# A new token order, a new order within the step, a new prologue, and one PSUM bank moved from one pool to another, in a fused sparse attention and MLP kernel

## The chip, the core and the metric

The kernel runs on one core of a Trainium2 chip. The metric is the time of one execution on the device, in microseconds (us), taken from repeated runs. The time before is 422.28 us (median of three runs, 421.58 to 422.75). The profiler names the engines PE (TensorE, matmuls), PEld (TensorE's weight loads, which overlap PE), DVE (VectorE), ACT (ScalarE), POOL (GpSimd, which issues the loads here) and SP (the queue that issues the stores).

## The reference, cut to what matters

```python
# q, k, v: (8 batches, 8 heads, 576 tokens, 64), float32
scores = (q @ k^T) / 8
mask_local   = 0 <= i - j < 32                       # heads 0 to 3
mask_strided = i >= j and i % 32 == j % 32           # heads 4 to 7
attn = softmax(where(mask, scores, -1e9)) @ v
x = attn as (4608 tokens, 512)
h = x @ w_in                                         # 512 -> 2048: "L1"
g = where(h > 0, h, exp(min(h, 0)) - 1)              # elu
out = g @ w_out                                      # 2048 -> 512: "L2"
```

## The kernel before

Attention is done by pairs of heads: per batch two strided pairs (`hp` 2 and 3), then two local ones (`hp` 0 and 1). A pair is three *pieces*: **T** transposes q and k on TensorE into a PSUM tile each, which VectorE copies to `qT` and `kT`; two **S** pieces compute the scores of one half each, take exp on ScalarE and multiply by the mask on VectorE. After each S comes its **PV**: TensorE computes the row sums (`s_ps`) and the unnormalized output (`o_ps`), ScalarE computes 1/s_ps as exp(-ln s_ps), and VectorE writes `xT = o_ps * rc`, bf16. `xT` holds the tokens as columns and is the moving operand of L1. For the strided heads a token number is 8 * row + slot (72 rows, 8 slots). 32 tokens are four rows, so tokens of different slots never attend to each other.

The main loop has 9 x 16 steps. Each computes one L1 block of 128 hidden units for 512 tokens (four matmuls of 512 columns) and a quarter of an L2 block of the previous 512 tokens (four more). One piece of attention is placed in each step until the pieces run out.

```python
p_s = tile_pool("ps_s", bufs=1, PSUM)    # scores, two banks
p_a = tile_pool("ps_a", bufs=2, PSUM)    # shared: transposes "tp", o_ps, s_ps
p_h = tile_pool("ps_h", bufs=2, PSUM)    # L1
p_o = tile_pool("ps_o", bufs=2, PSUM)    # L2
...
def piece_O(P, u, pm):                   # PV
    o_ps = p_a.tile([128, W], F32, tag="a")
    s_ps = p_a.tile([128, W], F32, tag="a")
    ... matmuls into s_ps, then into o_ps ...
    nc.scalar.activation(ln, s_ps, ACT.Ln)
    nc.scalar.activation(rc, ln, ACT.Exp, scale=-1.0)
    xs = xT[:, P.hp, P.b * S:(P.b + 1) * S]
    if P.str:      # columns are token numbers: rows p are 8 elements apart
        dst = xs.rearrange("c (p u sp z) -> c u z sp p", u=2, sp=2, z=2)[:, u]
        nc.vector.tensor_mul(dst, o_ps..., rc...)
    else:
        nc.vector.tensor_mul(xs[:, u * W:(u + 1) * W], o_ps, rc)
...
def run_piece(p):                        # the piece, then PV of the S before it
    old = list(pend); pend.clear()
    if u < 0: piece_T(...)
    else:     pend.append((..., piece_S(...)))
    for a in old: piece_O(*a)
...
for nb in range(NCH):                    # 9 blocks of 512 tokens
    for m in range(MC):                  # 16 steps
        run_piece(pieces[done]) ...      # if any is left
        l1(nb, m)
        if nb > 0: l2(nb - 1, m)
```

The softmax here doesn't subtract the row's maximum and nothing guards it: scores larger than these inputs give would overflow.

Of the kernel before, what the change touches and what calls it, by code (L numbers as in the profile page):

```python
# [9 lines left out]
F32 = mybir.dt.float32  # L10
BF16 = mybir.dt.bfloat16
# [17 lines left out]
def kernel(  # L29
# [22 lines left out]
    p_wk = ctx.enter_context(tc.tile_pool(name="work", bufs=3))  # L52
    p_g = ctx.enter_context(tc.tile_pool(name="g", bufs=2))
    p_s = ctx.enter_context(tc.tile_pool(name="ps_s", bufs=1, space=bass.MemoryType.PSUM))
    p_a = ctx.enter_context(tc.tile_pool(name="ps_a", bufs=2, space=bass.MemoryType.PSUM))
    p_h = ctx.enter_context(tc.tile_pool(name="ps_h", bufs=2, space=bass.MemoryType.PSUM))
    p_o = ctx.enter_context(tc.tile_pool(name="ps_o", bufs=2, space=bass.MemoryType.PSUM))

    ctx.enter_context(tc.manual_schedule())

# [7 lines left out]
            out=t, in_=src[b, HG:2 * HG].rearrange("h (p s) d -> p h (s d)", s=NS))  # L68
        return t

    def load_loc(src, b, name):

        t = p_in.tile([LQ, 2, LB, 2, D], BF16, tag=name, name=name)
        for h in range(HG):
            nc.gpsimd.dma_start(  # L75
                out=t[:, h // 2, :, h % 2, :],
                in_=src[b, h].rearrange("(t p) d -> p t d", p=LQ))
        return t
# [11 lines left out]
    def load_batch(b):  # L90
        t = {}
        t["qs"] = load_str(q, b, "qs")
        t["ks"] = load_str(k, b, "ks")
        t["vs"] = load_str(v, b, "vs")
        t["ql"] = load_loc(q, b, "ql")
        t["kl"] = load_loc(k, b, "kl")
        t["vl"] = load_vloc(b)
        return t

    batch_in = {}  # L100
    batch_in[0] = load_batch(0)

    w_in_sb = weights.tile([128, KC, d_ff], BF16, tag="w_in_sb")
    w_out_sb = weights.tile([128, MC, d_model], BF16, tag="w_out_sb")
    w_in_v = moe_w_in.rearrange("(kc p) f -> p kc f", p=128)
    w_out_v = moe_w_out.rearrange("(mc p) f -> p mc f", p=128)
    xT = weights.tile([128, KC, n_tokens], BF16, tag="xT")


    identity = consts.tile([128, 128], BF16, tag="identity")  # L110
# [4 lines left out]
    )  # L115
    ones = consts.tile([128, D], BF16, tag="ones")
    nc.vector.memset(ones, 1.0)



# [7 lines left out]
    mask_s = consts.tile([RS, RS], BF16, tag="mask_s")  # L128
    nc.vector.scalar_tensor_tensor(mask_s, dist, float(RS), eq, op0=ALU.is_ge, op1=ALU.mult)


    mask_l = consts.tile([128, LB, LQ], BF16, tag="mask_l")
    nc.vector.memset(mask_l, 1.0)
    nc.gpsimd.affine_select(
        mask_l, mask_l, compare_op=ALU.is_ge, fill=0.0,
        base=-1, pattern=[[0, LB], [-1, LQ]], channel_multiplier=1)
    nc.gpsimd.affine_select(
        mask_l, mask_l, compare_op=ALU.is_ge, fill=0.0,
        base=PRE, pattern=[[0, LB], [1, LQ]], channel_multiplier=-1)
    nc.vector.memset(mask_l[0:PRE, 0, :], 0.0)  # L140

    NT = 3
    KW = PRE + S - RS + 128
    kTs = [consts.tile([128, KW], BF16, tag=f"kT{i}", name=f"kT{i}") for i in range(NT)]
    qTs = [consts.tile([128, S], BF16, tag=f"qT{i}", name=f"qT{i}") for i in range(NT)]
    for t in kTs:
        nc.vector.memset(t[:, 0:PRE], 0.0)
        nc.vector.memset(t[:, PRE + S:], 0.0)

    for i in range(4):  # L150
        nc.gpsimd.dma_start(out=w_in_sb[:, :, i * 512:(i + 1) * 512],
# [22 lines left out]
    def piece_T(P):  # L174



        for nm, dst in (("q", P.qT[:, 0:S]), ("k", P.kT[:, PRE:PRE + S])):
            ps = p_a.tile([128, S], BF16, tag="a", name="tp")
            if P.str:  # L180
                src = batch_in[P.b][nm + "s"]
                for x in range(2):
                    for sp in range(NS // 2):
                        o = (x * (NS // 2) + sp) * RS
                        nc.tensor.transpose(  # L185
                            ps[:, o:o + RS],
                            src[:, P.g0 + x, 2 * sp * D:2 * (sp + 1) * D],
                            identity[0:RS, 0:RS])
            else:
                src = batch_in[P.b][nm + "l"]  # L190
                for t in range(LB):
                    nc.tensor.transpose(  # L192
                        ps[:, t * LQ:(t + 1) * LQ],
                        src[:, P.g0 // 2, t].rearrange("p h d -> p (h d)"),
                        identity[0:LQ, 0:LQ])
            nc.vector.tensor_copy(dst, ps)  # L196

    W = S // 2

    def piece_S(P, u):  # L200

        sc = p_s.tile([128, 2, 512], F32, tag="s", name="sc")
        pm = p_wk.tile([128, 2, W], BF16, tag="pm", name="pm")
        e = p_wk.tile([128, 2, W], BF16, tag="e", name="e")
        for i in range(4 if P.str else 3):
            for z in range(2):
                pr = slice(z * D, (z + 1) * D)
                if P.str:
                    x, sp = divmod(i, 2)
                    n = RS  # L210
                    o = (x * (NS // 2) + 2 * u + sp) * RS
                    k0 = PRE + o
                else:
                    n = LQ
                    o = (3 * u + i) * LQ
                    k0 = o
                nc.tensor.matmul(  # L217
                    sc[:, z, i * n:(i + 1) * n], lhsT=P.kT[pr, k0:k0 + 128],
                    rhs=P.qT[pr, o:o + n], start=True, stop=True)
        R = RS if P.str else 128  # L220
        nc.scalar.activation(e[0:R], sc[0:R, :, 0:W], ACT.Exp, scale=scale)  # L221
        if P.str:
            nc.vector.tensor_mul(  # L223
                pm[0:R].rearrange("p z (i n) -> p (z i) n", n=RS),
                e[0:R].rearrange("p z (i n) -> p (z i) n", n=RS),
                mask_s.unsqueeze(1).to_broadcast([RS, 8, RS]))
        else:
            mb = mask_l[:, 3 * u:3 * u + 3].rearrange("p b n -> p (b n)")
            nc.vector.tensor_mul(pm, e, mb.unsqueeze(1).to_broadcast([128, 2, W]))  # L229
        return pm  # L230

    def piece_O(P, u, pm):
# [36 lines left out]
        nc.scalar.activation(rc, ln, ACT.Exp, scale=-1.0)  # L269
        xs = xT[:, P.hp, P.b * S:(P.b + 1) * S]  # L270
        if P.str:

            dst = xs.rearrange("c (p u sp z) -> c u z sp p", u=2, sp=2, z=2)[:, u]
            pat = "c (z sp p) -> c z sp p"
            nc.vector.tensor_mul(dst, o_ps.rearrange(pat, z=2, sp=2),  # L275
                                 rc.rearrange(pat, z=2, sp=2))
        else:
            nc.vector.tensor_mul(xs[:, u * W:(u + 1) * W], o_ps, rc)  # L278


    pieces = []
    for b in range(B):
        for hp in (2, 3, 0, 1):
            pieces.append((b, hp, -1))
            for u in range(2):
                pieces.append((b, hp, u))
    pend = []
    cur = [None]

    def flush():  # L290
        while pend:
            P, u, pm = pend.pop(0)
            piece_O(P, u, pm)

    def run_piece(p):
        b, hp, u = p
        old = list(pend)
        pend.clear()
        if u < 0:
            cur[0] = make_pair(b, hp)  # L300
            piece_T(cur[0])
        else:
            pm = piece_S(cur[0], u)
            pend.append((cur[0], u, pm))
        for a in old:
            piece_O(*a)


    g_of = {}
# [1 line left out]
    def l1(nb, m):  # L311
# [14 lines left out]
                                op0=ALU.min, op1=ALU.subtract)  # L326
        nc.vector.tensor_tensor(g[:, m, :], e1, hps, op=ALU.max)  # L327

    o_cur = [None]

    def l2(nb, step):

        kk, part = divmod(step, 4)
        g = g_of[nb]
        if part == 0:
            o_cur[0] = p_o.tile([128, d_model], F32, tag="o", name="ops")
        ops = o_cur[0]
        for m in range(part * 4, part * 4 + 4):
            nc.tensor.matmul(  # L339
                ops, lhsT=g[:, m, kk * 128:(kk + 1) * 128],  # L340
                rhs=w_out_sb[:, m, :], start=(m == 0), stop=(m == MC - 1))
        if part == 3:
            o_sb = p_wk.tile([128, d_model], F32, tag="osb", name="osb")
            nc.scalar.copy(o_sb, ops)  # L344
            r0 = nb * CHUNK + kk * 128
            nc.sync.dma_start(out=out[r0:r0 + 128, :], in_=o_sb)


    n_p = len(pieces) // B
    done = 0  # L350
    while done < n_p:
        run_piece(pieces[done])
        done += 1
    AHEAD = 2
    for _ in range(AHEAD):
        run_piece(pieces[done])
        done += 1
    loaded = 2
    for nb in range(NCH):
        for m in range(MC):  # L360
            if done < len(pieces):
                run_piece(pieces[done])
                done += 1
            else:
                flush()
            l1(nb, m)
            if nb > 0:
                l2(nb - 1, m)
            if done % n_p == 6 and loaded < B and loaded <= done // n_p + 1:
                batch_in[loaded] = load_batch(loaded)  # L370
                loaded += 1
    for m in range(MC):
        l2(NCH - 1, m)


# [28 lines left out]
```

## Time and profile before

| stretch | us | what it is |
|---|---|---|
| 0 to 44.3 | 44.3 | fill: attention of batch 0 (and two pieces of batch 1) until the first L1 |
| 44.3 to 93.4 | 49.1 | first block: 16 steps with a piece and L1, no L2 |
| 93.4 to 297.6 | 204.2 | mixed: 67 steps with L1, L2 and attention |
| 297.6 to 402.9 | 105.3 | pure: 61 steps with L1 and L2 only |
| 402.9 to 421.6 | 18.7 | last L2 block, last copy and store |

The stretches are cut where the timeline shows the first L1, the first L2, the end of the last attention step, and the last L1. Here is the page of the kernel before (busy us and share of the span, and two of its rows of 40 equal slices, where a digit is tenths).

```profile
span 421.6 us, 6645 instructions
PE 345.6 (82%) x2584; PEld 171.2 (41%) x2624; DVE 271.7 (64%) x501; ACT 196.7 (47%) x373; POOL 88.9 (21%) x120
PE   0256776678888878888887888888999999999996
PEclk9999988989988998998999889899999999999999
```

The windows view of the same kernel gives the busy time of each engine in four of these stretches. The columns are the stretch, its length, PE, PEld, DVE, ACT and POOL busy, the granted TensorE clock, the DMA share, and GB/s.

```profile
0.00:44.30 44.30, 16.96 (x226) 13.08 (x228) 17.30 (x43) 14.73 (x29) 30.42 (x46) 1.00 1.33 139
44.30:93.40 49.10, 35.11 (x321) 17.88 (x326) 37.37 (x69) 24.00 (x49) 19.70 (x26) 0.89 1.39 126
93.40:297.60 204.20, 173.98 (x1494) 85.98 (x1516) 147.40 (x266) 109.24 (x214) 38.77 (x49) 0.93 0.46 55
297.60:402.90 105.30, 104.83 (x480) 47.73 (x488) 68.27 (x123) 45.19 (x76) 0.00 (x0) 1.00 0.10 38
```

Only the pure steps are bound by TensorE: it is busy 104.83 of 105.30 us, and a step takes 105.3 / 61 = 1.73 us. In the mixed steps nothing is full: TensorE idles for 30 us (about 4 of them only look idle, because 22 matmul records are missing from the trace), VectorE for 57, and the clock is 0.93. A busy average of 85% doesn't say what to do; the order of waits does. One T step on the timeline of the kernel before shows it (start, duration, engine, line, operation, output<-input; in brackets the engine's idle time just before, and what ended it).

```profile
202.68 1.45 DVE L275 TENSOR_TENSOR xT<-o_ps,rc 128x288 bf16<-128x288 f32 x1 [0.32 <-ACT rc L269]
203.23 0.42 PE L192 MATMUL tp<-identity,ql 96*128 96x96 bf16 x6
...
204.18 0.41 PE L192 MATMUL tp<-identity,kl 96*128 96x96 bf16 x6 [0.53 <-DVE xT L275]
...
205.06 0.42 DVE L196 COPY qT_130<-tp 128x576 bf16<-128x576 bf16 x1
205.39 0.45 DVE L196 COPY kT_127<-tp 128x576 bf16<-128x576 bf16 x1
205.53 0.31 PE L240 MATMUL s_ps<-pm,ones 72*64 72x288 bf16 x2 [0.94 <-DVE qT_130 L196]
...
205.89 0.32 PE L249 MATMUL o_ps<-pm,vs 72*64 72x72 bf16 x8
```

The K transposes (line 192, `kl`) wait for xT of the PV before, because that PV's `o_ps` holds one of the two shared banks. Then both shared banks hold transposes, so `s_ps` waits for the Q copy and `o_ps` for the K copy. L1, which needs neither, stands behind them in TensorE's queue and starts only at 206.37.

The groups view of the kernel before shows the two xT writes (count, busy us, mean ns, idle before). They move the same 128 x 288 elements.

```profile
L275 DVE TENSOR_TENSOR xT<-o_ps,rc 128x288 bf16<-128x288 f32 x32 | 46.0, 1437 | 20.0 <-ACT rc L269 20.0
L278 DVE TENSOR_TENSOR xT<-o_ps,rc 128x288 bf16<-128x288 f32 x32 | 14.6, 458 | 19.0 <-ACT rc L269 19.0
```

Line 275, the strided one, puts one bf16 into every 16 bytes and takes 1437 ns instead of 458.

### The profile page before, as it was taken

Reading aid. Unit: us, or ns where it says so; the run is one execution under the profiler, and the core shown is the slowest. Engines: PE = TensorE matmul, PEld = TensorE weight load, DVE = VectorE, ACT = ScalarE, POOL = GpSimd, SP = SyncE. Lnnn points to the kernel's source line nnn. Section 1 sums busy time; section 2 is a strip of 40 time slices with the busy share of each in tenths; the row PEclk is TensorE's granted clock in tenths of the full one; section 3 lists DMA queues with packets and bytes.
Section 4 is the critical chain, followed back from the end, with each engine's and each line's share of the span. In section 5 each row is a group of like instructions: output and inputs, shape, how many; then the busy total and the mean of one; then the engine's idle time right before and its main releaser. Section 6 shows DMA issues by size and latency. Waiting matters only on the chain.

```text
span 421.6 us, 6645 instructions
## 1 busy us (share of the span) xinstructions
PE 345.6 (82%) x2584; PEld 171.2 (41%) x2624; DVE 271.7 (64%) x501; ACT 196.7 (47%) x373; POOL 88.9 (21%) x120
## 2 busy tenths in 40 slices
PE   0256776678888878888887888888999999999996
PEld 0234433334433434443443344344444444444442
DVE  0265687786777777677777666776766666666620
ACT  1135454545644644564564446456543434444421
POOL 7847347404310530341051000000000000000000
PEclk9999988989988998998999889899999999999999
DMA  9999999925942964498296000000010101010111
GB/s 106 108 205 138 188 147 133 110 40 53 89 83 55 80 66 79 43 84 103 55 82 63 24 3 26 26 25 26 26 47 29 52 25 50 26 50 26 51 50 75
DMA packets 81502, 28.97 MB, mean 69 GB/s; under 512 B 65856, under 2 KB 76864, under 8 KB 81472
## 3 DMA queue, kind: packets, MB, share of 16 engines
q0 software_dynamic: 76288, 19.12, 49.7%
q1 hardware_dynamic: 5184, 9.44, 5.9%
q8 instruction: 20, 0.33, 0.3%
q14 instruction: 10, 0.08, 0.1%
HBM read 38.21 MB, written 9.44 MB: 113 GB/s over the span
## 4 chain that ended last, share of the span: by engine, by line
PE 61%; DVE 15%; DMA 9%; ACT 6%; issue 4%; POOL 4%; POOLq 0%; ACTq 0%
PE hps L318 28%; PE ops L339 27%; DVE xT L275 4%; DVE g L327 4%; DMA ks<-in_k_dram 3%; DMA qs<-in_q_dram 3%; PE sc L217 3%; ACT he L323 2%; DMA vs<-in_v_dram 2%; PE o_ps L261 1%; ACT e L221 1%; ACT rc L269 1%; PE o_ps L249 1%; PE s_ps L256 1%; ACT osb L344 1%
## 5 line engine op out<-in xcount | busy, mean ns | idle before, releaser
L318 PE MATMUL hps<-xT,w_in_sb 128*128 128x512 bf16 x542 | 152.4, 403 | 5.5 <-issue 5.2
L339 PE MATMUL ops<-w_out_sb,g 128*128 128x512 bf16 x570 | 151.0, 392 | 0.4
L323 ACT ACTIVATE he<-hps 128x512 f32<-128x512 f32 x144 | 85.8, 596 | 87.3 <-PE hps L318 84.4
L339 PEld LDWEIGHTS <-g 128*128 128x128 bf16 x576 | 58.0, 101 | 72.6 <-issue 8.2
L318 PEld LDWEIGHTS <-w_in_sb 128*128 128x128 bf16 x576 | 51.4, 101 | 58.5 <-issue 8.0
L221 ACT ACTIVATE e<-sc 72x576 bf16<-72x576 f32 (+1 forms) x64 | 41.4, 648 | 42.6 <-PE sc L217 41.3
L275 DVE TENSOR_TENSOR xT<-o_ps,rc 128x288 bf16<-128x288 f32 x32 | 46.0, 1437 | 20.0 <-ACT rc L269 20.0
L267 ACT ACTIVATE ln<-s_ps 128x288 f32<-128x288 f32 x64 | 26.1, 407 | 68.9 <-PE s_ps L240 39.1
L75 POOL DMA_DIRECT2D ql<-in_q_dram x32 | 23.6, 747 | 38.4 <-PE tp L192 27.2
L344 ACT COPY osb<-ops 128x512 f32<-128x512 f32 x36 | 21.1, 585 | 20.0 <-PE ops L339 20.0
L269 ACT ACTIVATE rc<-ln 128x288 f32<-128x288 f32 x64 | 28.3, 443 | 2.0
L75 POOL DMA_DIRECT2D kl<-in_k_dram x32 | 23.8, 755 | 16.5 <-DMA qs<-in_q_dram 6.2
L278 DVE TENSOR_TENSOR xT<-o_ps,rc 128x288 bf16<-128x288 f32 x32 | 14.6, 458 | 19.0 <-ACT rc L269 19.0
L240 PE MATMUL s_ps<-pm,ones 72*64 72x288 bf16 x64 | 11.0, 330 | 15.0 <-DVE qT_131 L196 4.9
L256 PE MATMUL s_ps<-pm,ones 128*64 128x288 bf16 x64 | 10.8, 327 | 13.2 <-DVE qT_130 L196 4.8
L223 DVE TENSOR_TENSOR pm<-e,mask_s 72x576 bf16<-72x576 bf16 x32 | 14.7, 459 | 8.2 <-ACT e L221 8.2
L185 PE MATMUL tp<-identity,qs 72*128 72x72 bf16 x128 | 7.7, 210 | 14.5 <-POOL identity L112 13.9
L229 DVE TENSOR_TENSOR pm<-e,mask_l 128x576 bf16<-128x576 bf16 x32 | 14.8, 463 | 4.4 <-ACT e L221 4.4
L67 POOL DMA_DIRECT2D vs<-in_v_dram x8 | 5.7, 716 | 45.0 <-PE o_ps L249 45.0
L185 PEld LDWEIGHTS <-qs 72*128 72x128 bf16 x128 | 7.1, 106 | 17.9 <-issue 8.3
L192 PE MATMUL tp<-identity,kl 96*128 96x96 bf16 x96 | 7.1, 214 | 7.7 <-DVE xT L275 7.0
L185 PE MATMUL tp<-identity,ks 72*128 72x72 bf16 x128 | 7.7, 210 | 6.8 <-DVE xT L275 6.2
(339 smaller groups left out, 349.4 us busy)
## 6 DMA issues: line engine op xcount, KB each, us to landing
out_dram<-osb SPq DMA_DIRECT2D x36, 256.0 KB, 2.0
qs<-in_q_dram POOLq DMA_DIRECT2D x8, 288.0 KB, 5.3
ks<-in_k_dram POOLq DMA_DIRECT2D x8, 288.0 KB, 6.4
vs<-in_v_dram POOLq DMA_DIRECT2D x8, 288.0 KB, 6.2
ql<-in_q_dram POOLq DMA_DIRECT2D x32, 72.0 KB, 4.9
kl<-in_k_dram POOLq DMA_DIRECT2D x32, 72.0 KB, 3.7
vl<-in_v_dram POOLq DMA_DIRECT2D x8, 288.0 KB, 5.2
w_in_sb<-in_moe_w_in_dram POOLq DMA_DIRECT2D x4, 512.0 KB, 8.2
```

What stands on the lines that cost most here:

```text
L75: nc.gpsimd.dma_start(out=t[:, h // 2, :, h % 2, :], in_=src[b, h].rearrange("(t p) d -> p t d", p=LQ))
L185: nc.tensor.transpose(ps[:, o:o + RS], src[:, P.g0 + x, 2 * sp * D:2 * (sp + 1) * D], identity[0:RS, 0:RS])
L221: nc.scalar.activation(e[0:R], sc[0:R, :, 0:W], ACT.Exp, scale=scale)
L256: nc.tensor.matmul(s_ps[x * D:(x + 1) * D, :], lhsT=ones, rhs=pm[:, x], start=True, stop=True, skip_group_check=True)
L267: nc.scalar.activation(ln, s_ps, ACT.Ln)
L269: nc.scalar.activation(rc, ln, ACT.Exp, scale=-1.0)
L275: nc.vector.tensor_mul(dst, o_ps.rearrange(pat, z=2, sp=2), rc.rearrange(pat, z=2, sp=2))
L318: nc.tensor.matmul(hps, lhsT=w_in_sb[:, cc, m * 128:(m + 1) * 128], rhs=xT[:, cc, nb * CHUNK:(nb + 1) * CHUNK], start=(c == 0), stop=(c == ...
L323: nc.scalar.activation(e, hps, ACT.Exp)
L327: nc.vector.tensor_tensor(g[:, m, :], e1, hps, op=ALU.max)
L339: nc.tensor.matmul(ops, lhsT=g[:, m, kk * 128:(kk + 1) * 128], rhs=w_out_sb[:, m, :], start=(m == 0), stop=(m == MC - 1))
L344: nc.scalar.copy(o_sb, ops)
```

## The change

The intent: (1) hold `xT` in the order (batch, slot, row), so that the strided write has runs of 72 elements; the local heads then write runs of 12, the local queries are read in that order, and the output rows are put back by the stores (96 instead of 36). (2) In each step run L2, then PV, then the piece, then L1, and transpose one pair ahead, so that TensorE always has work that waits for nothing. (3) Give the shared pool a third PSUM bank, taken from L2. (4) A prologue with the identity ahead of the loads, a deeper pipeline, and a second buffer for scores. The diff, cut to its core:

```diff
-    p_a = ctx.enter_context(tc.tile_pool(name="ps_a", bufs=2, space=bass.MemoryType.PSUM))
+    p_a = ctx.enter_context(tc.tile_pool(name="ps_a", bufs=3, space=bass.MemoryType.PSUM))
-    p_o = ctx.enter_context(tc.tile_pool(name="ps_o", bufs=2, space=bass.MemoryType.PSUM))
+    p_o = ctx.enter_context(tc.tile_pool(name="ps_o", bufs=1, space=bass.MemoryType.PSUM))
 ... (q of the local heads is loaded by slots; identity and kT edges are made before the first load;
 ...  vs, mask, ql, kl, vl of batch 0 follow; mask_l in the order block, slot, row;
 ...  the two pieces of batch 1 ahead of the loop go; later batches are loaded at another step;
 ...  the last L2 block alternates between its own bank and a shared one)
-                for t in range(LB):
+                n = RS if nm == "q" else LQ
+                for t in range(S // n):
 ...
-    def piece_S(P, u):
-        sc = p_s.tile([128, 2, 512], F32, tag="s", name="sc")
+    def piece_S(P, u, split=False):
+        if split:
+            scs = [p_h.tile([128, CHUNK], F32, tag="h", name="sc_h") for _ in range(2)]
+        else: ...
 ...
+                    rhs = P.qT[pr, :].rearrange("c (s p) -> c s p", s=NS)[
+                        :, :, p0:p0 + LQ // NS]
 ...
-            dst = xs.rearrange("c (p u sp z) -> c u z sp p", u=2, sp=2, z=2)[:, u]
+            dst = xs.rearrange("c (u sp z p) -> c u z sp p", u=2, sp=2, z=2)[:, u]
 ...
-            nc.vector.tensor_mul(xs[:, u * W:(u + 1) * W], o_ps, rc)
+            pat = "c (b s p) -> c b s p"
+            dst = xs.rearrange("c (s b p) -> c b s p", s=NS, b=LB)[:, 3 * u:3 * u + 3]
+            nc.vector.tensor_mul(dst, o_ps.rearrange(pat, b=3, s=NS), rc.rearrange(pat, b=3, s=NS))
 ...
+        pieces.append(("S", P, 0))
+        if (i + 1) % (H // 2):
+            pieces.append(("T", pairs[i + 1], 0))
+        pieces.append(("S", P, 1))
 ...
+    def run_piece(p, lag=0, split=False):
+        kind, P, u = p
+        flush(lag)                       # PV of what is pending, first
+        if kind == "T": piece_T(P)
+        else: pend.append((P, u, piece_S(P, u, split)))
 ...
     for nb in range(NCH):
         for m in range(MC):
+            if nb > 0:
+                l2(nb - 1, m)
             if done < len(pieces):
-                run_piece(pieces[done])
+                run_piece(pieces[done], lag=1 if nb == 0 else 0)
 ...
             l1(nb, m)
-            if nb > 0:
-                l2(nb - 1, m)
```

More of the change, by code (lines that the diff above doesn't have):

```diff
@@ L69, in load_str, with load_qloc, load_kloc @@
         return t
-    def load_loc(src, b, name):
+    def load_qloc(b):
+        t = p_in.tile([RS, 2, NS, 2, D], BF16, tag="ql", name="ql")
+        for h in range(HG):
+            nc.gpsimd.dma_start(
+                out=t[:, h // 2, :, h % 2, :],
+                in_=q[b, h].rearrange("(p s) d -> p s d", s=NS))
+        return t
+    def load_kloc(src, b, name):
         t = p_in.tile([LQ, 2, LB, 2, D], BF16, tag=name, name=name)
@@ L94, in load_batch @@
         t["vs"] = load_str(v, b, "vs")
-        t["ql"] = load_loc(q, b, "ql")
-        t["kl"] = load_loc(k, b, "kl")
+        t["ql"] = load_qloc(b)
+        t["kl"] = load_kloc(k, b, "kl")
         t["vl"] = load_vloc(b)
         return t
-    batch_in = {}
-    batch_in[0] = load_batch(0)
-    w_in_sb = weights.tile([128, KC, d_ff], BF16, tag="w_in_sb")
-    w_out_sb = weights.tile([128, MC, d_model], BF16, tag="w_out_sb")
-    w_in_v = moe_w_in.rearrange("(kc p) f -> p kc f", p=128)
-    w_out_v = moe_w_out.rearrange("(mc p) f -> p mc f", p=128)
-    xT = weights.tile([128, KC, n_tokens], BF16, tag="xT")
     identity = consts.tile([128, 128], BF16, tag="identity")
@@ L117 @@
     nc.vector.memset(ones, 1.0)
+    NT = 3
+    KW = PRE + S - RS + 128
+    kTs = [consts.tile([128, KW], BF16, tag=f"kT{i}", name=f"kT{i}") for i in range(NT)]
+    qTs = [consts.tile([128, S], BF16, tag=f"qT{i}", name=f"qT{i}") for i in range(NT)]
+    for t in kTs:
+        nc.vector.memset(t[:, 0:PRE], 0.0)
+        nc.vector.memset(t[:, PRE + S:], 0.0)
+    batch_in = {0: {}}
+    t0 = batch_in[0]
+    t0["qs"] = load_str(q, 0, "qs")
+    t0["ks"] = load_str(k, 0, "ks")
     dist = consts.tile([RS, RS], I32, tag="dist")
@@ L129 @@
     nc.vector.scalar_tensor_tensor(mask_s, dist, float(RS), eq, op0=ALU.is_ge, op1=ALU.mult)
-    mask_l = consts.tile([128, LB, LQ], BF16, tag="mask_l")
+    t0["vs"] = load_str(v, 0, "vs")
+    mask_l = consts.tile([128, LB, NS, LQ // NS], BF16, tag="mask_l")
     nc.vector.memset(mask_l, 1.0)
@@ L135 @@
         mask_l, mask_l, compare_op=ALU.is_ge, fill=0.0,
-        base=-1, pattern=[[0, LB], [-1, LQ]], channel_multiplier=1)
+        base=-1, pattern=[[0, LB], [-1, NS], [-NS, LQ // NS]], channel_multiplier=1)
     nc.gpsimd.affine_select(
         mask_l, mask_l, compare_op=ALU.is_ge, fill=0.0,
-        base=PRE, pattern=[[0, LB], [1, LQ]], channel_multiplier=-1)
+        base=PRE, pattern=[[0, LB], [1, NS], [NS, LQ // NS]], channel_multiplier=-1)
     nc.vector.memset(mask_l[0:PRE, 0, :], 0.0)
-    NT = 3
-    KW = PRE + S - RS + 128
-    kTs = [consts.tile([128, KW], BF16, tag=f"kT{i}", name=f"kT{i}") for i in range(NT)]
-    qTs = [consts.tile([128, S], BF16, tag=f"qT{i}", name=f"qT{i}") for i in range(NT)]
-    for t in kTs:
-        nc.vector.memset(t[:, 0:PRE], 0.0)
-        nc.vector.memset(t[:, PRE + S:], 0.0)
+    t0["ql"] = load_qloc(0)
+    t0["kl"] = load_kloc(k, 0, "kl")
+    t0["vl"] = load_vloc(0)
+    w_in_sb = weights.tile([128, KC, d_ff], BF16, tag="w_in_sb")
+    w_out_sb = weights.tile([128, MC, d_model], BF16, tag="w_out_sb")
+    w_in_v = moe_w_in.rearrange("(kc p) f -> p kc f", p=128)
+    w_out_v = moe_w_out.rearrange("(mc p) f -> p mc f", p=128)
+    xT = weights.tile([128, KC, n_tokens], BF16, tag="xT")
     for i in range(4):
@@ L190, in piece_T @@
                 src = batch_in[P.b][nm + "l"]
-                for t in range(LB):
+                n = RS if nm == "q" else LQ
+                for t in range(S // n):
                     nc.tensor.transpose(
-                        ps[:, t * LQ:(t + 1) * LQ],
+                        ps[:, t * n:(t + 1) * n],
                         src[:, P.g0 // 2, t].rearrange("p h d -> p (h d)"),
-                        identity[0:LQ, 0:LQ])
+                        identity[0:n, 0:n])
             nc.vector.tensor_copy(dst, ps)
     W = S // 2
-    def piece_S(P, u):
-        sc = p_s.tile([128, 2, 512], F32, tag="s", name="sc")
+    def piece_S(P, u, split=False):
+        if split:
+            scs = [p_h.tile([128, CHUNK], F32, tag="h", name="sc_h") for _ in range(2)]
+        else:
+            sc = p_s.tile([128, 2, 512], F32, tag="s", name="sc")
+            scs = [sc[:, 0], sc[:, 1]]
         pm = p_wk.tile([128, 2, W], BF16, tag="pm", name="pm")
@@ L212, in piece_S @@
                     k0 = PRE + o
+                    rhs = P.qT[pr, o:o + n]
                 else:
                     n = LQ
-                    o = (3 * u + i) * LQ
-                    k0 = o
+                    k0 = (3 * u + i) * LQ
+                    p0 = k0 // NS
+                    rhs = P.qT[pr, :].rearrange("c (s p) -> c s p", s=NS)[
+                        :, :, p0:p0 + LQ // NS]
                 nc.tensor.matmul(
-                    sc[:, z, i * n:(i + 1) * n], lhsT=P.kT[pr, k0:k0 + 128],
-                    rhs=P.qT[pr, o:o + n], start=True, stop=True)
+                    scs[z][:, i * n:(i + 1) * n], lhsT=P.kT[pr, k0:k0 + 128],
+                    rhs=rhs, start=True, stop=True)
         R = RS if P.str else 128
-        nc.scalar.activation(e[0:R], sc[0:R, :, 0:W], ACT.Exp, scale=scale)
+        if split:
+            for z in range(2):
+                nc.scalar.activation(e[0:R, z], scs[z][0:R, 0:W], ACT.Exp, scale=scale)
+        else:
+            nc.scalar.activation(e[0:R], sc[0:R, :, 0:W], ACT.Exp, scale=scale)
         if P.str:
@@ L227, in piece_S @@
         else:
-            mb = mask_l[:, 3 * u:3 * u + 3].rearrange("p b n -> p (b n)")
+            mb = mask_l[:, 3 * u:3 * u + 3].rearrange("p b s n -> p (b s n)")
             nc.vector.tensor_mul(pm, e, mb.unsqueeze(1).to_broadcast([128, 2, W]))
@@ L277, in piece_O, with flush @@
         else:
-            nc.vector.tensor_mul(xs[:, u * W:(u + 1) * W], o_ps, rc)
-    pieces = []
-    for b in range(B):
-        for hp in (2, 3, 0, 1):
-            pieces.append((b, hp, -1))
-            for u in range(2):
-                pieces.append((b, hp, u))
-    pend = []
-    cur = [None]
-    def flush():
-        while pend:
-            P, u, pm = pend.pop(0)
-            piece_O(P, u, pm)
-    def run_piece(p):
-        b, hp, u = p
-        old = list(pend)
-        pend.clear()
-        if u < 0:
-            cur[0] = make_pair(b, hp)
-            piece_T(cur[0])
-        else:
-            pm = piece_S(cur[0], u)
-            pend.append((cur[0], u, pm))
-        for a in old:
-            piece_O(*a)
+            pat = "c (b s p) -> c b s p"
+            dst = xs.rearrange("c (s b p) -> c b s p", s=NS, b=LB)[:, 3 * u:3 * u + 3]
+            nc.vector.tensor_mul(dst, o_ps.rearrange(pat, b=3, s=NS),
+                                 rc.rearrange(pat, b=3, s=NS))
+    pairs = [make_pair(b, hp) for b in range(B) for hp in (2, 3, 0, 1)]
+    pieces = []
+    for i, P in enumerate(pairs):
+        if i % (H // 2) == 0:
+            pieces.append(("T", P, 0))
+        pieces.append(("S", P, 0))
+        if (i + 1) % (H // 2):
+            pieces.append(("T", pairs[i + 1], 0))
+        pieces.append(("S", P, 1))
+    pend = []
+    def flush(keep=0):
+        while len(pend) > keep:
+            piece_O(*pend.pop(0))
+    def run_piece(p, lag=0, split=False):
+        kind, P, u = p
+        flush(lag)
+        if kind == "T":
+            piece_T(P)
+        else:
+            pend.append((P, u, piece_S(P, u, split)))
     g_of = {}
@@ L327, in l1, with store, l2 @@
         nc.vector.tensor_tensor(g[:, m, :], e1, hps, op=ALU.max)
+    out_v = out.rearrange("(b p s) f -> b s p f", b=B, s=NS)
+    def store(c0, o_sb):
+        c = c0
+        while c < c0 + 128:
+            b, r = divmod(c, S)
+            s, p = divmod(r, RS)
+            n = min(RS - p, c0 + 128 - c)
+            nc.sync.dma_start(out=out_v[b, s, p:p + n, :],
+                              in_=o_sb[c - c0:c - c0 + n, :])
+            c += n
     o_cur = [None]
-    def l2(nb, step):
+    def l2(nb, step, spare=False):
         kk, part = divmod(step, 4)
@@ L335, in l2 @@
         if part == 0:
-            o_cur[0] = p_o.tile([128, d_model], F32, tag="o", name="ops")
+            pool, tag = (p_a, "a") if spare and kk % 2 else (p_o, "o")
+            o_cur[0] = pool.tile([128, d_model], F32, tag=tag, name="ops")
         ops = o_cur[0]
@@ L344, in l2 @@
             nc.scalar.copy(o_sb, ops)
-            r0 = nb * CHUNK + kk * 128
-            nc.sync.dma_start(out=out[r0:r0 + 128, :], in_=o_sb)
-    n_p = len(pieces) // B
+            store(nb * CHUNK + kk * 128, o_sb)
+    PB = 3 * (H // 2)
     done = 0
-    while done < n_p:
-        run_piece(pieces[done])
+    while done < PB:
+        kind, P, u = pieces[done]
+        run_piece(pieces[done], lag=1, split=(kind == "S" and u == 1))
         done += 1
-    AHEAD = 2
-    for _ in range(AHEAD):
-        run_piece(pieces[done])
-        done += 1
+    flush()
     loaded = 2
@@ L360 @@
         for m in range(MC):
+            if nb > 0:
+                l2(nb - 1, m)
             if done < len(pieces):
-                run_piece(pieces[done])
+                run_piece(pieces[done], lag=1 if nb == 0 else 0)
                 done += 1
@@ L366 @@
             l1(nb, m)
-            if nb > 0:
-                l2(nb - 1, m)
-            if done % n_p == 6 and loaded < B and loaded <= done // n_p + 1:
+            if loaded < B and done >= (loaded - 1) * PB + 4:
                 batch_in[loaded] = load_batch(loaded)
@@ L372 @@
     for m in range(MC):
-        l2(NCH - 1, m)
+        l2(NCH - 1, m, spare=True)
 _INS = ['q', 'k', 'v', 'moe_w_in', 'moe_w_out']
```

## The prediction

> **What bounds it now.** The windows view shows three regimes.
> (1) 0 to 93 us: fill, plus the first 16 steps, which have no L2.
> (2) 93 to 297 us: 66 steps with an attention piece and L2. 3.09 us a step.
> (3) 297 to 421.6 us: 62 pure MLP steps at 1.73 us (8 matmuls at 216 ns, TensorE 99% busy); then 14 us of L2, copy, store.
> Only (3) is TensorE-bound. A pair in (2) (T, S, S) holds about 6.9 us of TensorE work (24 matmuls at 216 ns, attention 1.75 from the chain of waits), yet the timeline shows about 10.9 us per strided pair and 8.4 to 9.2 per local one. The rest: waits in the T step. The K transposes wait for a shared bank held by o_ps until VectorE writes xT (up to 1.6 us), then s_ps waits for the Q/K copies (0.9 to 1.4 us). The strided xT write takes 1437 ns against 458 for the contiguous one of equal size. The Trainium skill, "SBUF — State Buffer", Specifications: 16-byte lines want two or more hits; this write puts one bf16 in each, and the trace agrees. Long waits also cost clock: after them matmuls run at 427 ns for some 3.4 us, in about ten windows with a granted clock of 0.71 to 0.93 (halving: "TensorE: Matmul & The Clock Gate", Part 1).
>
> **What changes.**
> - Strided xT writes become runs of 72, local ones runs of 12: 460 to 500 ns for both, 31 us of VectorE work saved (32 x 0.97).
> - L2 and PV come before T, so PV no longer waits for the Q/K copies. T runs ahead.
> - Three shared banks: o_ps, s_ps, tpq, then tpk, which lands on o_ps again. So a wait remains in each T step: ln, rc, xT (0.41+0.44+0.46 us) less what TensorE does meanwhile, about 1 us.
> - One L2 bank: the 0.58 us copy fits beside L1's 0.86: 0 to 1 us in total.
> - 32 more small transposes (1 us); 96 stores, not 36, hidden but for 0.3 us.
> - Prologue: identity before the loads, so the first transposes run at about 7 us instead of 13.9; deeper pipelining, short writes: 4 to 4.5 us a pair instead of 5.2 to 6.6. First L1 at about 30 us instead of 44, two pieces fewer done.
>
> **Sum (estimates).**
> First L1 30. Sixteen steps at 2.1 (VectorE: 6.1 us a pair) = 34, plus 4 for loads of batch 1 and 2 (the DMA queue was full until about 57 us) and cold clock: 68. Then 68 steps at 8.05/3 = 2.68 us: 183, to 251. 60 steps at 1.73 plus 1: 105, to 356. Last block 14, ending 4: 374.
> About 24 us come from fill and first block, 23 from mixed steps, all on the critical path.
>
> **Predicted: 374 us, 80% range 360 to 391.** Faster by over 2%: 0.97; within: 0.02; slower: 0.01.
>
> **What would show it.** Both xT groups below 520 ns; no s_ps wait for Q/K copies; K transposes waiting 1 us for xT in each T step; mixed steps 2.5 to 2.8 us; granted clock near 1.00 in them; pure steps 1.73 to 1.76; first L1 at 27 to 34 us; VectorE busy near 240 us.
>
> **What would make it wrong.** Loads of batch 1 and 2 later than pieces want them; half clock through the first block (+10 us); runs of 12 slow to write or to stream; no bank wait in T (down to about 355 us).

## The result

The changed kernel takes 362.75 us (median of four runs, 361.38 to 363.2), against 422.51 us for the kernel before in the same rounds. The ratio is 0.8583, with a 95% interval of 0.8555 to 0.861. All ratios in this text are the mean time of one kernel's fast runs over the mean of the other's fast runs of the same rounds, so they are not quite the ratio of the medians.

The page of the changed kernel:

```profile
span 361.1 us, 6843 instructions
PE 329.1 (91%) x2656; PEld 161.5 (45%) x2656; DVE 243.8 (68%) x501; ACT 194.3 (54%) x377; POOL 92.3 (26%) x120
PEclk9999999899999999999999999999999999999999
```

Its windows, cut at the same events. The fill is shown in two rows, up to the end of batch 0's attention and from there to the first L1; the last row shown is the pure steps.

```profile
0.00:25.50 25.50, 13.46 (x188) 9.62 (x188) 12.24 (x39) 12.43 (x29) 19.84 (x30) 1.00 1.20 122
25.50:36.30 10.80, 1.11 (x16) 0.94 (x17) 0.50 (x2) 0.00 (x0) 3.31 (x5) 1.00 1.67 180
36.30:69.10 32.80, 27.68 (x288) 13.71 (x286) 26.50 (x58) 19.71 (x41) 19.56 (x25) 0.95 1.68 143
69.10:241.00 171.90, 170.89 (x1633) 84.82 (x1632) 137.15 (x283) 115.08 (x229) 49.60 (x62) 1.00 0.79 83
241.00:343.00 102.00, 102.00 (x474) 46.20 (x473) 66.01 (x120) 44.15 (x75) 0.00 (x0) 1.00 0.13 37
```

| stretch | before, us | after, us | difference |
|---|---|---|---|
| fill | 44.3 | 36.3 | -8.0 |
| first block | 49.1 | 32.8 | -16.3 |
| mixed | 204.2 (67 steps) | 171.9 (69 steps) | -32.3 |
| pure | 105.3 (61 steps) | 102.0 (59 steps) | -3.3 |
| last L2, copy, store | 18.7 | 18.1 | -0.6 |

Two pieces of attention are no longer done ahead of the first L1, so part of the 8.0 us is work that moved, and two steps moved from pure to mixed.

The mixed steps are now bound by TensorE: 170.89 of 171.90 us busy at the full clock. They fall from 204.2 / 67 = 3.05 us a step to 171.9 / 69 = 2.49.

The groups view of the changed kernel has both xT writes (304 strided, 309 local, now runs of 12) at the speed of a contiguous one:

```profile
L304 DVE TENSOR_TENSOR xT<-o_ps,rc 128x288 bf16<-128x288 f32 x32 | 14.6, 456 | 8.3 <-ACT rc L299 7.9
L309 DVE TENSOR_TENSOR xT<-o_ps,rc 128x288 bf16<-128x288 f32 x32 | 14.6, 457 | 7.8 <-ACT rc L299 5.0
```

A T step on the timeline of the changed kernel, the counterpart of the one shown before:

```profile
192.57 0.31 PE L270 MATMUL s_ps<-pm,ones 72*64 72x288 bf16 x2
...
192.93 0.41 ACT L297 ACTIVATE ln<-s_ps 128x288 f32<-128x288 f32 x1 [0.52 <-PE s_ps L270]
...
192.95 0.43 PE L211 MATMUL tp<-identity,ql 72*128 72x72 bf16 x8
...
193.39 0.41 PE L211 MATMUL tp<-identity,kl 96*128 96x96 bf16 x6
...
193.64 1.03 PE L347 MATMUL hps<-xT,w_in_sb 128*128 128x512 bf16 x4
193.85 0.46 DVE L304 TENSOR_TENSOR xT<-o_ps,rc 128x288 bf16<-128x288 f32 x1 [0.25 <-ACT rc L299]
```

PV comes first and waits for no copy. The Q transposes start at 192.95, before ln (which reads `s_ps`) ends at 193.34 and xT (which reads `o_ps`) at 194.31, so they are in the third bank. The K transposes follow at 193.39 and don't wait for xT. So the bank that they take is that of `s_ps`.

What TensorE still waits for in this kernel comes almost wholly before the first L2. In the waits view of PE (us in total, times, longest):

```profile
PE tp L203 <- DMA qs<-in_q_dram: 18.4, 3, 9.4
PE tp L203 <- DMA ks<-in_k_dram: 3.6, 3, 1.4
```

### The profile page after: what moved, and what is told of

Its sections match the earlier page's. It is cut to its first block, busy times and chain, and to the rows that moved or that the text cites. A ratio compares the mean times of both kernels' runs of the same rounds, so it can differ in the third digit from the quotient of the medians.

```text
span 361.1 us, 6843 instructions
## 1 busy us (share of the span) xinstructions
PE 329.1 (91%) x2656; PEld 161.5 (45%) x2656; DVE 243.8 (68%) x501; ACT 194.3 (54%) x377; POOL 92.3 (26%) x120
## 4 chain that ended last, share of the span: by engine, by line
PE 73%; DMA 12%; ACT 6%; POOL 4%; issue 2%; DVE 2%; ACTq 0%
PE ops L382 32%; PE hps L347 30%; DMA vs<-in_v_dram 5%; DMA ks<-in_k_dram 5%; PE tp L211 3%; PE tp L203 2%; PE sc L243 2%; ACT e L251 2%; ACT osb L387 2%; DMA vl<-in_v_dram 2%; DVE pm L259 2%; PE s_ps L286 1%; ACT ln L297 1%; PE s_ps L270 1%; POOL kl L85 1%
## 5 line engine op out<-in xcount | busy, mean ns | idle before, releaser
L382 PE MATMUL ops<-w_out_sb,g 128*128 128x512 bf16 x576 | 145.4, 379 | 0.0
L382 PEld LDWEIGHTS <-g 128*128 128x128 bf16 x576 | 56.4, 98 | 68.0
L251 ACT ACTIVATE e<-sc 72x576 bf16<-72x576 f32 (+1 forms) x60 | 38.3, 639 | 17.4 <-PE sc L243 17.4
L76 POOL DMA_DIRECT2D ql<-in_q_dram x32 | 27.2, 855 | 18.0 <-PE tp L211 6.6
L304 DVE TENSOR_TENSOR xT<-o_ps,rc 128x288 bf16<-128x288 f32 x32 | 14.6, 456 | 8.3 <-ACT rc L299 7.9
L309 DVE TENSOR_TENSOR xT<-o_ps,rc 128x288 bf16<-128x288 f32 x32 | 14.6, 457 | 7.8 <-ACT rc L299 5.0
L203 PEld LDWEIGHTS <-qs 72*128 72x128 bf16 x128 | 5.8, 108 | 19.9 <-DMA qs<-in_q_dram 18.7
L96 POOL DMA_DIRECT2D vl<-in_v_dram x8 | 9.6, 1197 | 11.8 <-PE tp L203 11.4
L291 PE MATMUL o_ps<-pm,vl 128*64 128x96 bf16 x192 | 10.6, 215 | 0.7 <-DMA vl<-in_v_dram 0.7
```

The costliest lines, as they stand in the source:

```text
L76: nc.gpsimd.dma_start(out=t[:, h // 2, :, h % 2, :], in_=q[b, h].rearrange("(p s) d -> p s d", s=NS))
L203: nc.tensor.transpose(ps[:, o:o + RS], src[:, P.g0 + x, 2 * sp * D:2 * (sp + 1) * D], identity[0:RS, 0:RS])
L251: nc.scalar.activation(e[0:R], sc[0:R, :, 0:W], ACT.Exp, scale=scale)
L304: nc.vector.tensor_mul(dst, o_ps.rearrange(pat, z=2, sp=2), rc.rearrange(pat, z=2, sp=2))
L382: nc.tensor.matmul(ops, lhsT=g[:, m, kk * 128:(kk + 1) * 128], rhs=w_out_sb[:, m, :], start=(m == 0), stop=(m == MC - 1))
```

## The experiments

The theory to test: the time came from TensorE's waits in the T step, and each of four parts (tokens, banks, order of the step, prologue) takes a share. The main rival: VectorE's shorter work is the whole gain. A second rival was in no expectation, but the traces can be asked for it: the half clock of TensorE in the kernel before. For each kernel the table gives the first L1, the first L2 and the last PV as the timeline shows them, and from these the time of a mixed step (from the first L2 to the last PV less about 0.9 us for one quarter of L2, over the number of steps in between: 65 for the three kernels made from the one before and for the kernel before itself, 67 for `old_step_order`, 68 for the rest; this cuts the stretch a little differently from the tables above).

| kernel | median us | ratio to before | first L1 | first L2 | last PV | us a mixed step |
|---|---|---|---|---|---|---|
| before | 422.51 | 1 | 44.3 | 93.2 | 296.3 | 3.11 |
| `tok_only`: before + tokens | 399.6 | 0.945 | 42.1 | 87.6 | 270.5 | 2.80 |
| `banks_only`: before + banks | 390.83 | 0.926 | 41.5 | 83.1 | 260.3 | 2.71 |
| `tok_banks`: before + both | 380.03 | 0.899 | 38.9 | 76.4 | 248.4 | 2.63 |
| after | 362.75 | 0.858 | 36.3 | 69.1 | 239.9 | 2.50 |
| `old_tokens`: after - tokens | 370.49 | 0.874 | 35.2 | 68.9 | 248.2 | 2.62 |
| `banks_2_2`: after - banks | 387.4 | 0.914 | 36.7 | 70.8 | 263.7 | 2.82 |
| `old_step_order`: after - order | 374.5 | 0.884 | 36.0 | 71.3 | 249.1 | 2.64 |
| `t_not_ahead` | 362.15 | 0.859 | 35.8 | 68.4 | 238.9 | 2.49 |
| `old_prologue` | 365.61 | 0.867 | 41.9 | 71.7 | 242.5 | 2.50 |
| `tpk_on_o` | 387.59 | 0.919 | 35.7 | 71.1 | 264.1 | 2.82 |
| `loads_mixed` | 351.89 | 0.835 | 27.4 | 56.9 | 231.1 | 2.55 |

All these kernels gave correct results. Each was timed in three rounds beside the kernel before, whose medians were 424.17, 423.04 (its one slow run included) and 422.87 us in the three batches.

### The new token order alone

```diff
# the kernel before, with: load_qloc, mask_l and local scores by slots,
-            dst = xs.rearrange("c (p u sp z) -> c u z sp p", u=2, sp=2, z=2)[:, u]
+            dst = xs.rearrange("c (u sp z p) -> c u z sp p", u=2, sp=2, z=2)[:, u]
# and the permuted stores; nothing else
```

> The kernel before with the new token order alone (old step order, banks and prologue). Theory (waits in the T step): the strided xT writes fall from 1437 to about 457 ns, so strided pairs fall to the 8.4 to 8.6 us of the local ones, but the waits of s_ps for the Q/K copies stay: about 25 us off the mixed steps and 8 off the fill, so about 390 us. Rival (the 31 us of VectorE work are the whole gain): 372 us or less.

Measured: 399.6 us, about 24 us less than before. TensorE's wait for xT all but vanishes from its waits view, and its wait of `s_ps` for the Q copy stays, 27.1 us in 27 times. The theory's direction holds, though it expected 10 us more. The rival, that VectorE's 31 us are the whole gain, falls. But the way is in good part another, as the windows view of the mixed steps shows, beside that of the kernel before:

```profile
87.60:271.40 183.80, 160.29 (x1515) 82.45 (x1537) 128.79 (x266) 108.91 (x214) 38.92 (x50) 1.00 0.54 62
```

Of the 20.4 us that the mixed steps lose, TensorE's idle time is 6.7 (30.2 to 23.5) and its busy time 13.7 (173.98 to 160.29, with as many records missing): the same matmuls, no longer at half clock. In the kernel before, the trace has eight stretches of about 3.4 us at half clock in the mixed steps, each just after a T step with two waits (0.76 and 0.92 us before the one at 233). With the Q-copy wait alone there is none.

### The old token order in the changed kernel

```diff
# the changed kernel with
+            dst = xs.rearrange("c (p u sp z) -> c u z sp p", u=2, sp=2, z=2)[:, u]
# old mask_l, old local q and plain stores
```

> The changed kernel with the old token order (strided writes of one bf16 in 16 bytes, plain stores); step order, banks and prologue new. Theory: VectorE has about 8.0 us of work in a strided pair against 7.5 us for TensorE, so it binds there a little: 9 us in the mixed steps and a few in the fill, about 375 us. Rival (token order is the whole gain): 400 us or more.

Measured: 370.49 us, 7.7 more than the changed kernel (the theory had 12), so with the rest of the change in place VectorE's shorter write is worth a third of what it was worth alone. VectorE is then busy 154.23 of the 180.60 us between 68.9 and 249.5, and TensorE again waits for the masked scores and xT. VectorE is 85% busy there, so that it binds, as the theory said, isn't shown.

### Two shared banks in the changed kernel

```diff
-    p_a = tile_pool(name="ps_a", bufs=3, ...)      -    p_o = tile_pool(name="ps_o", bufs=1, ...)
+    p_a = tile_pool(name="ps_a", bufs=2, ...)      +    p_o = tile_pool(name="ps_o", bufs=2, ...)
```

> The changed kernel with two shared banks and two L2 banks, all else new. Theory: in a T step the Q transposes wait for s_ps (ln) and the K transposes for o_ps (xT), 1.0 to 1.3 us a T step, 22 of them in the mixed steps: about 385 to 390 us. Rival (the order of the step does it, not the banks): 366 us or less.

Measured: 387.4 us, 24.7 more, as the theory has it. A step goes from 2.50 to 2.82 us; a pair is three steps, so that is about 1.0 us for each T step. PV waits for the Q copy 0.2 us in all; T waits instead, 26.1 us for ln and xT. The second bank of L2, by contrast, bought nothing: the pure steps of both kernels take 1.73 us.

### The old order of the step in the changed kernel

```diff
-            if nb > 0: l2(nb - 1, m)
-            run_piece(...)            # PV of what is pending, then the piece
+            run_piece_old(...)        # the piece, then PV
             l1(nb, m)
+            if nb > 0: l2(nb - 1, m)
```

> The changed kernel with the old order in the loop's steps (piece, its PV after it, L1, L2); T still one pair ahead, three shared banks, new tokens and prologue. Theory: s_ps in a T step again waits for the Q copy, about 0.9 us a T step: about 382 us, with TensorE waiting for the qT and kT copies in the waits view. Rival (banks and tokens do it): 368 us or less.

Measured: 374.5 us, 11.8 more. The expected 382 was too much. It isn't `s_ps` that waits now but `o_ps`, for 0.5 us a time (13.5 us in 27 times). Its releaser is ln, and not the Q copy: each of the 27 times `o_ps` starts 0.05 us after the ln of its own PV ends, and at least 0.05 us before the Q copy ends. So `o_ps` takes the bank that `s_ps` of the same PV has just left. With a third bank the old order costs half as much as with two (0.94 us in the T step shown before).

### T in its old place

```diff
-        pieces.append(("S", P, 0))
-        if (i + 1) % (H // 2): pieces.append(("T", pairs[i + 1], 0))
+        pieces.append(("T", P, 0)); pieces.append(("S", P, 0))
         pieces.append(("S", P, 1))
```

> The changed kernel with the pieces of a pair in the order T, S, S again (T no longer one pair ahead). Theory: the copies after T have L1 and L2 of the step, 1.73 us, before the scores want them, so no new wait: 361 to 366 us. Rival (running T ahead is what hides the copies): 375 us or more.

Measured: 362.15 us, the same as the changed kernel. Running T one pair ahead brings nothing here: a step's L1 and L2 already cover the copies.

### The old prologue in the changed kernel

```diff
# all loads of batch 0 ahead of the identity and the masks, and
-        run_piece(pieces[done], lag=1, split=(kind == "S" and u == 1))
+        run_piece(pieces[done])
```

> The changed kernel with the prologue of before: all loads of batch 0 ahead of the identity, PV right after the next piece, one score buffer. Theory (after the prologue TensorE waits for the loads of batch 1 until 33.8 us anyway, and for batch 2 until 60.6): the first transposes fall back to about 13.9 us and the prologue ends near 38, but the first block still ends near 70 us: 362 to 367 us. Rival (the fill's gain is the prologue's own): 370 us or more.

Measured: 365.61 us, 2.9 more. The first L1 comes 5.6 us later, the first L2 only 2.6 us later. That is the theory: the new prologue ends its work at 25.5 us and then TensorE waits for the loads of batch 1, so most of what the prologue gains is given back. Most of the 24 us that fill and first block got shorter are not its doing: with the old prologue they take 71.7 us, against 93.4 in the kernel before.

### The K transposes on the bank of o_ps

```diff
-    p_a = tile_pool(name="ps_a", bufs=3, ...)
+    p_a = tile_pool(name="ps_a", bufs=2, ...)      # s_ps and the Q transposes
+    p_b = tile_pool(name="ps_b", bufs=1, ...)      # o_ps and the K transposes
```

> The changed kernel with the bank of the K transposes forced onto that of o_ps, as the prediction had assumed; the Q transposes and s_ps share the other two. Theory: the K transposes wait for xT, about 1 us a T step as predicted, so the mixed steps take about 2.7 us instead of 2.5 and the run 374 to 383 us. Rival (the time saved against the prediction lies elsewhere): 365 us or less.

This kernel puts the K transposes where the prediction had assumed them. It also leaves `o_ps` that one bank alone, which the prediction did not. Measured: 387.59 us, 24.8 more than the changed kernel and above the 374 to 383 expected. In its waits view PE waits for xT before the K transposes (203 to 213 are its lines of T):

```profile
PE tp L213 <- DVE xT L306: 8.6, 10, 1.1
PE tp L205 <- DVE xT L311: 6.6, 6, 1.7
PE tp L213 <- DVE xT L311: 5.8, 6, 1.0
PE tp L205 <- DVE xT L306: 4.9, 5, 1.0
```

That is 25.9 us in 27 waits, 0.96 us each. `o_ps` itself waits for xT of the PV before, 4.0 us in 8 times. The predicted wait of about 1 us was right for this place of the K transposes; the changed kernel doesn't have them there. A third bank is worth as much as its place: with three banks, one of them misplaced, the kernel is as slow as with two.

### The banks alone, and banks with tokens

```diff
# the kernel before, and tok_only, each with
-    p_a = tile_pool(name="ps_a", bufs=2, ...)      -    p_o = tile_pool(name="ps_o", bufs=2, ...)
+    p_a = tile_pool(name="ps_a", bufs=3, ...)      +    p_o = tile_pool(name="ps_o", bufs=1, ...)
```

> The kernel before with three shared banks and one L2 bank, nothing else. Theory: the K transposes get s_ps's bank, so their wait for xT (15 us in the whole run before, up to 1.6 us each) goes; the wait of s_ps for the Q copy stays, because the old order puts PV after T: about 15 us less, near 407 us. Rival (banks are the main part whatever the order, as undoing them cost 25 us): 398 us or less. Second rival (banks help only together with the new order): 418 us or more.

> The kernel before with the new token order and with three shared banks and one L2 bank, old step order and prologue. Theory (parts add up as undone from the other end: order 12 us, prologue 3, T ahead 0): about 378 us. Rival (the parts only work together): 390 us or more.

Two digits of the source make 32 us: 390.83 us. The theory for `banks_only` fell and its first rival holds. I had taken the wait of `s_ps` for the Q copy for a matter of order. It was also a matter of banks: with two, both PV tiles had to take the banks that the transposes had just filled; with three, neither does. `s_ps` takes the third, and `o_ps` follows it there once ln has read it, as in this T step of `banks_only`, where the Q copy hasn't even begun:

```profile
179.81 0.31 PE L240 MATMUL s_ps<-pm,ones 72*64 72x288 bf16 x2 [0.27 <-DVE xT L275]
180.16 0.41 ACT L267 ACTIVATE ln<-s_ps 128x288 f32<-128x288 f32 x1 [0.51 <-PE s_ps L240]
...
180.62 0.32 PE L249 MATMUL o_ps<-pm,vs 72*64 72x72 bf16 x8 [0.50 <-ACT ln L267]
...
180.69 0.42 DVE L196 COPY qT<-tp 128x576 bf16<-128x576 bf16 x1
```

The waits view of PE in `banks_only` shows what is left, with the slow xT still in it:

```profile
PE s_ps L240 <- DVE xT L275: 9.0, 15, 1.1
PE o_ps L249 <- ACT ln L267: 7.0, 14, 0.5
PE o_ps L261 <- ACT ln L267: 6.5, 13, 0.5
```

`tok_banks` takes 380.03 us, as expected from the parts undone at the other end. So the change adds up like this: banks alone 32 us, tokens alone 24, both together 43, and order and prologue the last 17. That both together are 13 us less than the sum is about what the half clock cost: 0.07 of the 204.2 us of mixed steps is 14 us, and each change alone brings the clock there to 1.00. That this is the whole overlap isn't shown. Measured from the other end, taking one part away costs 25 us for the banks, 12 for the order, 8 for the tokens, 3 for the prologue and nothing for T.

### How the run length of a write counts

```diff
# wrong result on purpose: only the targets of the strided xT writes differ
+ hp 2, u 0: xs[:, 0:W].rearrange("c (p m r) -> c m p r", m=4, r=2)     # runs of 2 per 16 bytes
+ hp 2, u 1: xs[:, W:2*W].rearrange("c (p m r) -> c m p r", m=2, r=4)   # runs of 4 per 16 bytes
+ hp 3, u 0: xs[:, 0:W].rearrange("c (p m) -> c m p", m=4)              # single, 8 bytes apart
+ hp 3, u 1: xs[:, W:2*W].rearrange("c (p m) -> c m p", m=2)            # single, 4 bytes apart
```

> Wrong result on purpose: the changed kernel, where only the target addresses of the strided xT writes differ, 288 bf16 each from the same PSUM source: runs of 2 per 16 bytes, runs of 4 per 16 bytes, single elements 8 bytes apart, single elements 4 bytes apart. The durations of these four lines are read from the trace. Theory (two hits in each 16-byte line suffice): all four near 457 ns, as runs of 72. Rival (every break of a run costs, or every new line): between 457 and 1437 ns, by the number of runs, so single elements 4 and 8 bytes apart slowest.

One look, with a wrong result, as intended. The view of the tile xT gives each line's durations in ns (minimum, median, maximum; lines 305, 310, 315 and 320 are the four targets in the order above; 325 is the local heads' write with runs of 12):

```profile
L325 DVE TENSOR_TENSOR xT<-o_ps,rc x32: 450/457/459, 20.7 to 241.2; 128x288 bf16<-128x288 f32 x32
L305 DVE TENSOR_TENSOR xT<-o_ps,rc x8: 421/457/459, 13.1 to 216.3; 128x288 bf16<-128x288 f32 x8
L310 DVE TENSOR_TENSOR xT<-o_ps,rc x8: 448/457/459, 14.4 to 221.2; 128x288 bf16<-128x288 f32 x8
L315 DVE TENSOR_TENSOR xT<-o_ps,rc x8: 790/798/806, 16.8 to 223.7; 128x288 bf16<-128x288 f32 x8
L320 DVE TENSOR_TENSOR xT<-o_ps,rc x8: 476/483/490, 18.1 to 228.9; 128x288 bf16<-128x288 f32 x8
```

Runs of 2 adjacent bf16 are already as fast as a contiguous write. Single elements take 483 ns at 4 bytes, 798 at 8 and (in the kernel before) 1437 at 16. Neither theory holds: two hits in a 16-byte line are enough when they are adjacent and not when they are 8 bytes apart, and the number of runs does not order the four either. What the memory does with such a write is left open. For this write, it is enough to keep two elements together.

### The loads in another order

```diff
-    w_in (4 parts); all of batch 1; w_out (4 parts); in step 4 of the loop: all of batch 2
+    w_in 0; qs, ks of batch 1; w_in 1; vs, ql, kl of batch 1; w_in 2; vl of batch 1; w_in 3;
+    after the prologue: qs, ks, vs of batch 2; w_out (4 parts); ql, kl, vl of batch 2
```

> The changed kernel with the loads reordered: the quarters of w_in between the tensors of batch 1, q, k and v of batch 2's strided heads ahead of w_out. Theory (order of the loads, not their amount, holds TensorE at 25 to 34 us and 58 to 62): first L1 at about 26 us instead of 36.3, first block done by about 60 instead of 69: about 353 us. Rival (the queue is full and the wait only moves to later loads): 360 us or more.

Measured: 351.89 us, the fastest kernel of this study (0.835 of before, where the changed kernel is at 0.858). The first L1 comes at 27.4 us instead of 36.3, the first L2 at 56.9 instead of 69.1. The same bytes are loaded; only what TensorE needs first comes first. Part of the 12 us is given back: the local q and k of batch 2 now arrive late, in the mixed steps, and PE waits for them.

```profile
PE tp L219 <- DMA kl<-in_k_dram: 1.5, 1, 1.5
PE tp L219 <- DMA ql<-in_q_dram: 0.3, 1, 0.3
```

After the wait for `kl` the next L1 group runs slower for a moment (1.59 us instead of 1.03 on the timeline), so the mixed steps come to 2.55 us instead of 2.50.

## Why the prediction was right

The measured 362.75 us lie in the range of 360 to 391 us, 11 us below the predicted 374. The range held by some luck: "no bank wait in T (down to about 355 us)" stood among what would make the prediction wrong, and it came about; too small an estimate of TensorE's own work made up for part of it. Point by point:

- **What bound the kernel: right.** Waits in the T step, and the half clock after them, bound the mixed steps; the granted clock there goes from 0.93 to 1.00. `tok_only` and `banks_only`, which keep part of the waits, are at 1.00 too, so the clock comes back before the waits are gone. The Trainium skill, "TensorE: Matmul & The Clock Gate", Part 1, describes a clock gate set by how busy TensorE has been just before. The trace agrees: half clock (matmuls of 427 instead of 216 ns) is visible in the kernel before and gone from the changed kernel's mixed steps.
- **Both xT writes below 520 ns: right.** They take 456 and 457 ns. VectorE is busy 243.8 us, predicted near 240.
- **First L1 at 27 to 34 us: wrong.** It comes at 36.3 us. The prologue itself is done at 25.5 us, faster than the predicted 30, but the next transposes wait 9.4 us for q of batch 1. The prediction had the wait for loads in its sum, as 4 us of the first block, and so met the end of that block (predicted 68, measured 69.1 us) by a wrong division. `loads_mixed` shows that the order of the loads is what holds TensorE there.
- **"tpk, which lands on o_ps again. So a wait remains in each T step ... about 1 us": wrong.** The K transposes land on the bank of `s_ps`, free once ln has read it, and in the mixed steps TensorE waits 0.2 us in all, and a step takes 2.49 us, just below the 2.5 to 2.8 predicted. `tpk_on_o` forces the assumed place and finds the assumed wait, 0.96 us. I had assumed that the pool goes round its banks in the order in which the program names the tiles (`o_ps`, `s_ps`, Q, K). The trace of before had a hint: there the Q transposes start at 203.23, while xT still reads `o_ps`, so they have the bank of `s_ps`, and the K transposes wait for xT. The pool gives out first the bank whose last reader comes first. `banks_only` and `old_step_order`, where `o_ps` follows `s_ps` of the same PV into its bank, fit this and no fixed round of three banks.
- **"about 6.9 us of TensorE work" in a pair: too small.** The mixed steps of the changed kernel are 99% TensorE and take 3 x 2.49 = 7.5 us a pair. Of that, 24 matmuls of 216 ns are 5.2, so attention costs about 2.3 us, not 1.75. The two errors have opposite signs: a wait of about 1 us that isn't there, and some 0.6 us of work that is. The predicted pair of 8.05 us became 7.47. Over the mixed steps that is 11 us (183 predicted, 171.9 measured), about the distance from the predicted 374.
- **"PV no longer waits for the Q/K copies" through the order of the step: right, but not the order's alone.** `banks_2_2` has the new order without the third bank, and 0.2 us of that wait is left; but then T waits, 26.1 us. `banks_only` has the third bank in the old order and loses that wait too. The third bank is worth more than the order (25 against 12 us when undone).
- **T runs ahead:** named as part of the cure; `t_not_ahead` shows that it does nothing.
- **One L2 bank costs 0 to 1 us: right.** A pure step takes 102.0 / 59 = 1.73 us, as before. **The end: right**, predicted 18 us, measured 18.1.

## What to carry to other kernels

When an engine waits for another engine's copy, and other work stands behind it in its queue, ask first which buffer it waits for: here one PSUM bank taken from a pool that didn't need it (the copy of 0.58 us fits beside the 0.86 us of L1) was worth 32 us alone, more than the layout change of 24 us or the reordered step. The Trainium skill, "Perfetto Trace Analysis", Optimization Strategy, says that the same gap repeating on the engine that should be full can mean too few buffers; the 0.9 us in 27 T steps of the kernel before were exactly that. And when a prologue gets faster, look at what it now waits for: its gain stayed with the loads until they were issued in the order of need.

## What the Trainium skill lacked or had wrong

- "SBUF — State Buffer", Specifications, asks for two or more hits in a 16-byte line for full bandwidth. For VectorE's bf16 write from PSUM two adjacent hits do it (457 ns, as contiguous), but two hits 8 bytes apart take 798 ns, and four hits 4 bytes apart 483; one hit takes 1437.
- "Perfetto Trace Analysis", Matmul Optimizations, asks for all eight PSUM banks to be in use. Every kernel here uses eight; how they are divided among the pools, and which tiles share a bank, makes 387.6 or 362.75 us.
- No page says which bank of a pool a new tile gets. The runs show that it is the one freed first (in the changed kernel the K transposes start at 193.39, after ln at 193.34 and before xT ends at 194.31; in `banks_only` `o_ps` starts 0.05 us after the ln of its own PV). The K transposes on the bank of `o_ps`, with `o_ps` on that bank alone, cost 25 us.
